# First batch's last three pairs of heads: token loads in 3072-byte pieces, with the cluster products taken by token parity

## The chip, the cores and the metric

The kernel runs on one core of a Trainium2 chip. A core has a matrix engine (TensorE, PE in the profile), a vector engine (VectorE, DVE), an engine for activation functions (ScalarE, ACT), a general engine (GpSimd, POOL), a queue engine that issues most DMA transfers (SyncE, SP), and sixteen DMA engines that all queues share. Each engine runs its own instructions strictly in order and waits for others by semaphores. The metric is the device time of one execution in microseconds; lower is better.

## The reference

Two stages follow each other. The first is attention in which a query sees only those keys that fall into its own cluster; the second is a feed-forward layer with a softmax-gated activation and a layer norm.

```python
batch, n_heads, seq, head_dim = (4, 8, 768, 64); n_clusters = 16
q_assign = np.argmax(np.einsum('bhsd,hcd->bhsc', q_n, c_n), axis=-1)
k_assign = np.argmax(np.einsum('bhsd,hcd->bhsc', k_n, c_n), axis=-1)
mask = q_assign[:, :, :, None] == k_assign[:, :, None, :]
scores = np.where(mask, scale * np.matmul(q, k.transpose(0, 1, 3, 2)), -1000000000.0)
attn = softmax(scores)
attn_out = np.matmul(attn, v)
x = attn_out.transpose(0, 2, 1, 3).reshape(B * S, H * D)      # 3072 x 512
h = x @ w_in                                                   # 3072 x 1024
solu = h * softmax(h)
ln = (solu - mu) / np.sqrt(var + 1e-06) * g_ln
return ln @ w_out                                              # 3072 x 512
```

All inputs and the output are 32-bit floats. q_n, k_n and c_n are the rows divided by their lengths.

## The kernel before

**Tiling.** The work is cut by batch (4) and by pairs of heads (4 in a batch), so there are 16 pairs; a name such as ca0.2.1.0 is a step, its batch, its pair, its side (0 for q, 1 for k) and a part. A pair's q and its k each fill one raw tile of 128 x 768 floats. What the attention needs is the transpose: the 64 head dimensions on partitions, the tokens as columns, in bf16, with 16 more rows below that hold each token's cluster as a one-hot column. These rows enter the same matrix product as the head dimensions, so that a score of a token pair from different clusters comes out so low that its exponential is nothing.

**The steps of a pair.** ld loads the raw tile. In the first batch (by_token) the six tokens of a partition lie beside each other and TensorE turns the tile by six 128x128 transposes into the region hreg (tp, L363), three a half; xa copies a half out of it (L370); in the other batches ld uses 128-byte pieces and VectorE turns 32x32 blocks (xt, L384). ca casts one head's 64 rows into the buffer qk (L400, L402, L404). cl multiplies the turned tile with the centroids (L413): four products that each write 32 rows of one output bank; the strips are q and k, first and second half of the tokens, and the weights c_bd hold both heads' centroids, zero outside their own head's rows. tb, mx, oh and ot (L422, L435, L440, L446) turn the result on VectorE, take the largest over 16 clusters, compare, and turn the one-hot columns back. pl puts them under both heads' columns of qk (L460, or L458 by a DMA), bl blanks 16 rows (L469). Then S makes the scores (TensorE, L539), E their exponentials (ScalarE, L545), V the sums over keys (L562), N divides (L587). The second stage is h (L648), its maximum hm, its exponential ex, the product u, statistics bn and ag, the transposes tx and tu by DMA, and y (L709).

**Before this stream.** The first pair of the first batch (halves_of) goes half by half, loaded ahead of everything else by SP and ScalarE. The centroids are normalised (cn), turned (cp, L796) and copied with a mask into c_bd (cb, L800). The weights of the second stage are loaded by lo and li, lo's are summed with the gains by VectorE (su, L514 and L517); their mean over 1024 rows is one matrix product (me, L522), which centres them (ce, L525). The values are loaded by lv and cast by cv (L478). fl are idle products that fill time.

**Order.** No scheduler decides the order of instructions. Every step is registered with a name, an engine, a cost and what it needs; for each engine a text (ORDER) lists the kinds of steps one after another, and each entry takes the next registered step of its kind on that engine. AWAY names the steps that run on another engine than their default. Both are long lists, and one change in them moves the whole order. Costs and the planned transfer times (move, lag) only decide in which order the engines' lists are merged as they are written out, not what an engine does first.

**Buffers that tie steps together.** raw has 8 tiles, xt 6, the scores' PSUM ring 3 banks, so that ScalarE can lag TensorE by three banks. hreg has three banks, used in turn by tp and later by h. One PSUM bank (tag m) is shared by cl, cp, the transpose of the gains (gt) and y: who takes it waits until it was read.

```python
eng.dma_start(out=tokens(b, p, i)[:, t0:t1, hh * D:(hh + 1) * D],
              in_=SRC[i][b, 2 * p + hh].rearrange("(p t) d -> p t d", p=P)[:, t0:t1, :])
```

This is the load of one head of the first batch: for each of 128 partitions six tokens in a row, but each token's 256 bytes go to a place of their own, since the other head's token lies between.

Of the kernel before, what the change touches and what calls it, by code (L numbers as in the profile page):

```python
# [22 lines left out]
class Weave:  # L23
# [6 lines left out]
        ld4 lv si ld11 lo lg ld lo lv ld2 lo ld3 lo ld2 lv ld3 lv ld3 li ld3 li2 ld2 li ld3 tx ld3  # L30
        lv ld3 lv ld5 tx2 lv tu ld3 tu ld lv ld9 tu ld4 lv ld6 tu2 ou2 tx lv ld3 tx ld tu ld ou lv
        tu ld6 ou ld7 tx ld5 ou ld2 lv ld2 ou ld6 ou tu ld4 tu2 lv ld pl2 tx ld2 ou ld lv2 tx lv pl
        tu2 pl tx ou2 pl3 tu2 ou tu ou tx2 tu ou tu tx tu ou tx tu ou tx ou2 tu ou tu2 ou6
    """
    ORDER["POOL"] = """
        po ca2 pl2 ca bl pl2 bl sg cv ca3 pl ca pl4 ca z bl z2 cv pl3 ca cv ca pl ca bl ca cv ca pl2
        ca pl cv pl ca cv ca cv pl2 ca wi pl wi z pl wi2 pl2 ca bl2 cv pl2 ca2 cv pl2 cv ca3 pl at z
        ca cv ca pl3 bl2 al at cv ca2 cv2 al pl ca pl ca at cv at ca3 pl3 al pl al ca6 at bl pl cv
        ca al pl3 cv2 at pl al ca2 bl ca pl2 at bl cv al pl ca at ca2 cv pl cv pl2 al pl at ca cv bl
        pl2 ca2 bl at ca3 al ca2 at cv at cv ca4 cv ca pl3 cv bl at pl al pl bl at al pl al at2 ca  # L40
        al pl cv at al2 at al3 at3 al2 at2 al2 at al2
    """
    ORDER["PE"] = """
        wm tp2 cp tp cl tp fl5 cl fl5 S3 tp S tp S2 tp2 S3 tp2 cl V tp2 V2 S3 cl S2 V3 S tp2 S2 gt
        S2 tp S2 V3 S2 tp S3 V S V S V S2 cl S3 V3 S2 V S2 V S V S4 V2 S V S2 V2 S2 V S2 me S2 V S
        V3 S2 V2 S3 cl S2 V S2 V2 S V2 S V S4 V S V3 S3 cl S3 V2 S V2 S3 V S2 V3 S2 h S h S2 h2 S3
        cl S V2 S V2 h V2 S h S2 h S h S2 V S V3 S V S V S h2 cl S2 h S h S2 V S V2 S h S2 V3 S2 y4
        S2 V2 S V2 S2 h V2 S2 h2 S2 y S V2 S y3 S3 V h2 S h S V h S V2 S2 h2 S2 V S V cl V2 S2 h V2
        S3 cl S2 V3 S2 V h S2 y S V2 S V2 S y S2 y2 h V S2 V h2 S V S h S2 h y S2 V y3 S2 V2 S h S
        V2 S V S h2 S2 V S cl h S V3 S2 h y V y S y S2 y V2 S h2 S3 V h V S y S y3 V3 h S V S2 y S y  # L50
        S2 V2 y S2 y S h V2 S2 h S V2 S2 cl S3 V2 cl h S2 V S V2 S h2 V S2 h S h S2 V cl V3 S2 V S y
        V y S3 y h S y V S V2 S2 y S V h S2 h S V2 S V2 S2 y2 S3 h2 V2 y S V2 S2 h3 S3 V h S V cl S2
        V2 S V cl S V S2 h S h V S V S y3 S2 V h V2 y S V S2 h S h S h S V2 S V S y2 h S y V2 y S V
        h S h3 S3 h V2 S2 V y S y2 V y V2 S2 h3 S3 V h y2 V y V S y V S3 h2 S V S V S y S V2 y S3 y2
        h2 S V h2 S3 h V y S V2 y3 S h S2 h V2 h S y S V2 y2 h S y S h V h S h S V S y V2 y S y S y
        h4 y4 h S h y4 S h2 V4 y3 ptx y h2 y h2 ptu2 y8 ptu2 y7
    """
    ORDER["DVE"] = """
        cn cb ca tb mx oh ot pl2 cv tb mx oh ot xa3 ca2 tb ca xa pl mx oh tb ot xa gk N su xa2 mx su
        oh xa ot N tb su3 mx N oh su3 N ot xt2 ce N ce bl xt tb mx oh ot N ce xt N ce4 tb N mx oh ot  # L60
        ce xt N xt hm tb mx u N oh ot hm xt2 u tb N mx oh hm bn2 ag bn ot N u xt bn N bn2 hm ag xt u
# [11 lines left out]
    """  # L73
    AWAY = {}
    AWAY.update(dict.fromkeys("""
        ca0.0.0.0.1 ca0.0.0.1.0 ca2.2.1.0 tu23.1 xa0.0.0.1 xa0.0.1.0 xa0.1.1.0 xa0.2.0.0 xa0.2.0.1
        xa0.2.1.1
    """.split(), "ACT"))
    AWAY.update(dict.fromkeys("""
# [90 lines left out]
def kernel(  # L170
# [176 lines left out]
    def halves_of(b, p):  # L347
        return (b, p) == (0, 0)
# [816 lines left out]
```

## Time and profile before

| | us |
|---|---|
| median of 3 runs | 229.61 (228.98 to 231.76) |
| profiled execution, device time | 230.08 |
| its span, first to last instruction | 227.7 |
| busy: TensorE, VectorE, ScalarE, GpSimd | 218.3, 198.0, 193.9, 131.4 |

The profiled execution thus has 2.4 us outside its span. Busy time of TensorE is that of pipelined matrix products, whose ends are modelled. Of the page's second part, which cuts the span into 40 slices of 5.7 us, three rows matter here: the busy tenths of TensorE, the clock that it was granted, and the share of the DMA engines.

```profile
PE   7997999999999999999999999999999999999993
...
PEclk9999799999999999999999999999999999999999
DMA  6999799999999989899989999599246317557513
```

The fifth slice, 22.8 to 28.5 us, has a granted clock of 0.7. The loads' shapes and what they took from issue to landing are in the page's last part; the rows with 192 KB are the loads of the first batch:

```profile
vf<-in_v_dram SPq DMA_DIRECT2D x16, 384.0 KB, 4.6
...
w_g<-in_moe_w_out_dram SPq DMA_DIRECT2D x4, 512.0 KB, 7.1
...
raw<-in_q_dram SPq DMA_DIRECT2D x6, 192.0 KB, 4.6
raw<-in_k_dram SPq DMA_DIRECT2D x6, 192.0 KB, 4.7
```

One line of the list of who waited for whom:

```profile
PE hreg L363 <- DMA raw<-in_k_dram: 1.9, 2, 1.4
```

This reads: TensorE stood before transposes of raw tiles for 1.9 us in total, two times, the longest 1.4 us, and what came last was a load of k.

### The profile page before, as it was taken

How to read it: one execution, taken by the hardware profiler on the slowest of the kernel's cores; microseconds unless marked ns; L12 is line 12 of the kernel's file. 1: busy time of each engine (PE TensorE's matmuls, PEld its weight loads, DVE VectorE, ACT ScalarE, POOL GpSimd, SP SyncE). 2: the span in 40 equal slices, each digit the busy share in tenths (PEclk: the TensorE clock that was granted, in tenths of full speed). 3: DMA queues.
4: the chain of work that ended last, by engine and by line, in shares of the span. 5: the costliest groups of instructions: out<-in, count | busy, mean ns of one | idle time of the engine just before them, and what ended most of it. 6: DMA issues, size and time to landing. Idle time of an engine off the chain costs nothing.

```text
span 227.7 us, 6584 instructions
## 1 busy us (share of the span) xinstructions
PE 218.3 (96%) x2404; PEld 149.1 (65%) x2404; DVE 198.0 (87%) x348; ACT 193.9 (85%) x376; POOL 131.4 (58%) x253
## 2 busy tenths in 40 slices
PE   7997999999999999999999999999999999999993
PEld 3554767666767866867667677766667676665552
DVE  2888689999999989999899997899997996988980
ACT  3776799999999999999998999999988897874462
POOL 2495596877775975598489084979542240141131
PEclk9999799999999999999999999999999999999999
DMA  6999799999999989899989999599246317557513
GB/s 154 253 227 279 158 243 210 232 192 191 189 186 164 200 132 208 194 200 217 190 143 208 181 208 166 107 199 198 53 140 124 96 32 156 137 120 210 156 69 121
DMA packets 133695, 38.95 MB, mean 171 GB/s; under 512 B 124376, under 2 KB 129184, under 8 KB 133664
## 3 DMA queue, kind: packets, MB, share of 16 engines
q1 hardware_dynamic: 131920, 38.01, 81.9%
q10 hardware_dynamic: 1744, 0.52, 0.9%
q8 instruction: 19, 0.31, 0.6%
q14 instruction: 12, 0.10, 0.1%
HBM read 23.11 MB, written 6.29 MB: 129 GB/s over the span
## 4 chain that ended last, share of the span: by engine, by line
PE 78%; DMA 5%; SPq 5%; issue 4%; ACT 4%; DVE 2%; ACTq 0%; DVEq 0%
PE sps L539 24%; PE hreg L648 18%; PE yps L709 16%; PE ops L562 13%; PE csc L413 4%; SPq L356 4%; ACT e L545 4%; DMA raw<-in_k_dram 3%; DMA out_dram<-y 1%; DMA raw<-in_q_dram 1%; PE hreg L363 1%; DVE y L726 0%; DVE nmax L654 0%; SPq L510 0%; DVE bs L676 0%
## 5 line engine op out<-in xcount | busy, mean ns | idle before, releaser
L545 ACT ACTIVATE e<-sps 128x512 bf16<-128x512 f32 (+1 forms) x294 | 151.5, 605 | 13.9 <-PE sps L539 13.0
L539 PE MATMUL sps<-qk 80*128 80x256 bf16 (+5 forms) x636 | 97.8, 265 | 1.8 <-POOL qk L460 0.4
L539 PEld LDWEIGHTS <-qk 96*128 96x128 bf16 (+1 forms) x636 | 61.2, 121 | 30.1 <-issue 10.4
L562 PEld LDWEIGHTS <-e 128*128 128x128 bf16 x1152 | 52.2, 98 | 10.3 <-issue 2.2
L562 PE MATMUL ops<-v,e 128*128 128x65 bf16 x1152 | 56.8, 194 | 0.0
L648 PE MATMUL hreg<-w_in_sb,xT 128*128 128x512 bf16 x192 | 53.1, 379 | 0.2 <-DVE xT L629 0.2
L709 PE MATMUL yps<-w_out_c,uT 128*128 128x512 bf16 x184 | 48.7, 378 | 0.0
L460 POOL COPY qk<-oht 32x384 f32<-32x384 f32 (+1 forms) x58 | 29.0, 499 | 32.2 <-DVE oht L446 24.1
L665 DVE TENSOR_TENSOR u<-e_sb,hreg 128x1024 bf16<-128x1024 bf16 x24 | 29.0, 1208 | 5.5 <-ACT e_sb L660 5.4
L660 ACT ACTIVATE e_sb<-hreg,nmax 128x1024 bf16<-128x1024 f32 x24 | 26.8, 1117 | 7.7 <-DVE nmax L654 6.0
L676 DVE BATCH_NORM_STATS2 bs<-u 128x6 f32<-128x512 bf16 x48 | 31.3, 675 | 0.2
L654 DVE TENSOR_REDUCE nmax<-hreg 128x1 f32<-128x1024 f32 x24 | 29.1, 1212 | 1.8 <-PE hreg L648 1.7
L402 POOL CAST qk<-xt 64x768 bf16<-64x768 f32 (+1 forms) x29 | 24.6, 849 | 6.1 <-ACT xt L370 3.4
L404 POOL TENSOR_SCALAR qk<-xt 64x768 bf16<-64x768 f32 (+1 forms) x30 | 25.2, 839 | 2.2 <-ACT xt L370 0.4
L709 PEld LDWEIGHTS <-uT 128*128 128x128 bf16 x200 | 17.9, 97 | 10.9
L648 PEld LDWEIGHTS <-xT 128*128 128x128 bf16 x192 | 16.8, 97 | 10.8 <-DVE xT L629 0.7
L384 DVE STREAM_TRANSPOSE xt<-raw 128x768 f32<-128x768 f32 x24 | 22.6, 956 | 0.0
L692 POOL TENSOR_SCALAR esq<-es,mv 128x1 f32<-128x1 f32 x24 | 8.2, 340 | 24.8 <-DVE mv L680 23.7
L587 DVE TENSOR_TENSOR x<-ops,den 128x384 bf16<-128x384 f32 (+1 forms) x37 | 18.6, 503 | 1.3
L478 POOL CAST v<-vf 128x384 bf16<-128x384 f32 x27 | 14.7, 549 | 4.6 <-PE ops L562 2.7
L686 POOL TENSOR_SCALAR es<-esum 128x1 f32<-128x1 f32 x24 | 5.2, 220 | 17.0 <-ACT e_sb L660 16.3
L695 POOL TENSOR_TENSOR alpha<-esq,halves 128x1 f32<-128x1 f32 x24 | 13.7, 571 | 2.0
(70 smaller groups left out, 164.7 us busy)
## 6 DMA issues: line engine op xcount, KB each, us to landing
vf<-in_v_dram SPq DMA_DIRECT2D x16, 384.0 KB, 4.6
out_dram<-y SPq DMA_DIRECT2D x23, 256.0 KB, 2.3
raw<-in_q_dram SPq DMA_DIRECT2D x50, 96.0 KB, 3.5
raw<-in_k_dram SPq DMA_DIRECT2D x50, 96.0 KB, 3.4
w_g<-in_moe_w_out_dram SPq DMA_DIRECT2D x4, 512.0 KB, 7.1
w_st<-in_moe_w_in_dram SPq DMA_DIRECT2D x4, 512.0 KB, 6.2
raw<-in_q_dram SPq DMA_DIRECT2D x6, 192.0 KB, 4.6
raw<-in_k_dram SPq DMA_DIRECT2D x6, 192.0 KB, 4.7
```

Of the source, the lines that this page charges most:

```text
L402: VEC[e].tensor_copy(dst, xt[r, cols])
L404: VEC[e].tensor_scalar(dst, xt[r, cols], scalar1=inv_C, scalar2=1.0, op0=Alu.mult, op1=Alu.mult)
L460: ins = VEC[e].tensor_copy(dst.bitcast(F32), src.bitcast(F32).unsqueeze(1) .to_broadcast([NB, 2, n // 2]))
L539: nc.tensor.matmul(sps_[n, k][:, c0:c0 + w], side(b, h // 2, 1, h % 2, keys)[r], side(b, h // 2, 0, h % 2, slice(s0 * P, s0 * P + w))[r])
L545: nc.scalar.activation(es[n, k][:, :w], sps_[n, k][:, :w], Act.Exp, scale=exp_scale, bias=-exp_scale)
L562: nc.tensor.matmul(opss[g][:, s, :VW], es[n, k][:, c0:c0 + P], v1[slot(b, h // 2)][:, h % 2, kt, :VW], start=(kt == 0), stop=(kt == n_t - 1))
L648: uses(nc.tensor.matmul(hreg[:, at(f, f2)[1], :], xTs[f][:, dc, :], w_in_sb[:, dc, f2 * FF2:(f2 + 1) * FF2], start=(dc == 0), stop=(dc == ...
L654: uses(nc.vector.tensor_reduce(ff[f, "nmax"][:], pair_of(f), axis=AXY, op=Alu.max, negate=True), *both(f))
L660: uses(nc.scalar.activation(ff[f, "e"][:], pair_of(f), Act.Exp, bias=ff[f, "nmax"][:], accum_out=ff[f, "esum"][:]), *both(f))
L665: uses(nc.vector.tensor_tensor(ff[f, "u"][:], ff[f, "e"][:], pair_of(f), op=Alu.mult), *both(f))
L676: nc.vector.bn_stats(ff[f, "bs"][:, f2, :], ff[f, "u"][:, f2, :])
L709: ins = nc.tensor.matmul(dst, ff[f, "uT"][:, at(f, f2)[0] * (n_fc // 2) + c, :], w_out_c[:, fc, cols], start=(fc == 0), stop=(fc == n_fc - 1))
```

## The change

For pairs 1, 2 and 3 of the first batch (twelve), the token tile is laid out in another way. Both heads' tokens go twelve by twelve on 64 partitions each, so that a partition's 3072 bytes are one run in memory and in the tile, and a side needs one load of 384 KB where it had two of 192 KB. A transpose of 128 columns now turns two neighbouring tokens of both heads: the rows that come out are token parity and head dimension, the columns are head and partition.

```diff
+    def load_twelve(b, p, i):
+        raws[b, p, i] = ld.tile([P, n_j, NB], F32, name="raw")
+        nc.sync.dma_start(out=raws[b, p, i][:].rearrange("p j c -> p (j c)"),
+                          in_=SRC[i][b, 2 * p:2 * p + 2].rearrange("h (q t) d -> (h q) (t d)",
+                                                                   q=D))
+    def by_two(b, p, i):
+        return xts[b, p, i][:].rearrange("p (h t n) -> p h t n", h=2, t=n_t // 2)
```

The copy out of hreg (xa) puts every column at every other place, so that the order of tokens in qk stays what it was. A cast (ca) now takes one parity of both heads and writes every other block of 128 columns; so the scores of either head need all four casts of their pair.

```diff
+        if twelve(b, p):
+            dst = by_two(b, p, i).rearrange("p h t (q u) -> p h t u q", u=2)[:, :, :, hf, :]
+            src = src.rearrange("p (t h q) -> p h t q", h=2, q=D)
...
+    def every_other(b, p, i, part):
+        return (qk[slot(b, p)][:, i * 2 * S:(i + 1) * 2 * S]
+                .rearrange("p (h t n) -> p h t n", h=2, t=n_t)[:, :, part::2, :])
...
+        if twelve(b, p):
+            src, dst = by_two(b, p, i)[r], every_other(b, p, i, hh)[:D]
```

The strips of the cluster product are now q and k, even and odd tokens. A strip sums two products, one for each head, with weights that are zero but for the rows of one parity and the columns of one head; there are eight products where there were four.

```diff
+        if twelve(b, p):
+            for hh, c in ((hh, c) for hh in range(2) for c in range(4)):
+                i, part = divmod(c, 2)
+                nc.tensor.matmul(csc[c * NB:(c + 1) * NB, :], c_by_two[:, p, 2 * part + hh, :],
+                                 by_two(b, p, i)[:, hh].rearrange("p t n -> p (t n)"),
+                                 start=(hh == 0), stop=(hh == 1), tile_position=(0, c * NB))
```

These weights, c_by_two, lie in the tile of the second stage's weights, which is not yet in use, and are made by a second transpose of the centroids (cq) and a product with a mask (cf), ahead of which GpSimd writes the mask with five memsets:

```diff
+    nc.gpsimd.memset(own_two, 0.0)
+    for part in range(2):
+        for hh in range(2):
+            nc.gpsimd.memset(own_two[part * D:(part + 1) * D, 2 * part + hh,
+                                     hh * NC_:(hh + 1) * NC_], 1.0)
...
+    def keep_by_two():
+        nc.vector.tensor_tensor(
+            c_by_two, cs["t"][:].rearrange("p a h c -> p a (h c)").unsqueeze(2)
+            .to_broadcast([P, n_pair, 4, 2 * NC_]),
+            own_two.unsqueeze(1).to_broadcast([P, n_pair, 4, 2 * NC_]), op=Alu.mult)
+    add("cq", "PE", 0.28, 0, lambda e: turn_centroids(), ["cn"], ["cp"], take="m")
+    add("cf", "DVE", 0.65, -490, lambda e: keep_by_two(), ["cq"], give="m")
```

Placing (pl) writes every other block as well, on GpSimd or VectorE.

ORDER and AWAY are new throughout, for all five engines and all batches. What they move in the first stretch, by name:

- SP: the six loads come first, with lv0.1 ahead of the last and lv0.2 ahead of lo0; lo0 to lo3 come after them, among the loads of batch 1. In all nine placings go by DMA (seven before).
- TensorE: cq stands ahead of the first scores S0.0; cl0.1 behind tp0.2.1.0, cl0.2 ahead of V1.0 and S2.0, gt ahead of tp0.3.0.0; from S3.0 to me the order is nearly what it was.
- VectorE: xa0.0.0.0, xa0.2.0.1, cf, cv0.1.1, pl0.1.0.1 and pl0.2.0.0 come to it; ca0.0.1.1.1 and ca0.2.0.0 leave it; ot0.3 stands ahead of su4 (before: behind su7).
- ScalarE: xa0.0.0.0 and xa0.2.0.1 leave it; ca0.1.0.0 comes to it, between E0.4 and E0.5; the first pair's casts stand ahead of and behind xa0.0.1.1.
- GpSimd: it has 208 steps in all where it had 218; cv0.0.0 stands ahead of the first placing.

More of the change, by code (lines that the diff above doesn't have):

```diff
@@ L46 @@
[L46 to L50, printed above, removed]
```

140 lines of the change are left out of this document (78 added, 62 removed).

## The prediction, on record before the changed kernel ran

> **What bounds the kernel now.** I read the page first, then the chain that ended last in order of time, then windows and the timeline of the first 40 us, where every edited step lies.
>
> ```profile
> PE 218.3 (96%) x2404; PEld 149.1 (65%) x2404; DVE 198.0 (87%) x348; ACT 193.9 (85%) x376; POOL 131.4 (58%) x253
> ```
>
> TensorE is the engine that the end stands on. Its idle time before raw tiles and its slow clock both lie early. The chain names the place:
>
> ```profile
> 12.87 0.79 SPq L356
> 13.71 1.02 SPq L510
> 15.23 6.54 DMA raw<-in_k_dram
> 21.91 0.78 PE hreg L363 x3
> ...
> 28.18 0.78 PE csc L413 x8
> ...
> 37.80 0.94 PE hreg L522 x2
> ```
>
> (start, us, what.) SP issues the token loads one by one at 0.65 to 0.9 us each; the last one, issued at 15.23 behind a weight load, takes 6.54 us to land, and TensorE starts its transpose only at 21.91. The windows (engines' busy us, granted clock, DMA share, GB/s) show what it cost:
>
> ```profile
> 12.00:16.00 4.00, 3.52 (x44) 2.29 (x42) 3.27 (x5) 2.74 (x8) 3.79 (x7) 1.00 1.32 220
> 16.00:20.00 4.00, 4.00 (x46) 2.37 (x43) 3.90 (x9) 3.23 (x8) 1.63 (x3) 1.00 1.11 318
> ...
> 20.50:21.00 0.50, 0.01 (x1) 0.00 (x0) 0.32 (x1) 0.50 (x3) 0.46 (x2) 1.00 1.10 341
> ...
> 22.00:22.50 0.50, 0.50 (x4) 0.44 (x5) 0.00 (x0) 0.00 (x0) 0.50 (x1) 0.53 0.37 67
> ...
> 25.00:25.50 0.50, 0.50 (x4) 0.43 (x3) 0.00 (x0) 0.50 (x2) 0.34 (x1) 0.55 1.19 200
> ```
>
> While 256-byte pieces are loaded the queue moves 220 GB/s at a full share; with 2048-byte weight rows in it, 318. TensorE stands from 20.51 to 21.91 (1.40 us) and then runs at half clock to 25.45, 3.45 us. So what the late load costs is 1.40 + 3.45/2 = 3.1 us. Two more windows, and VectorE's and ScalarE's rows:
>
> ```profile
> 14.80:37.60 22.80, 20.60 (x244) 14.56 (x242) 19.07 (x34) 18.12 (x40) 16.54 (x26) 0.93 0.94 222
> 26.00:58.00 32.00, 30.55 (x398) 21.62 (x400) 29.60 (x52) 31.07 (x63) 25.34 (x38) 1.00 0.96 201
> ```
>
> ```profile
> 14.82 0.58 DVE L422 STREAM_TRANSPOSE cst<-csc 128x384 f32<-128x384 f32 x1 [0.50 <-PE csc L413]
> ...
> 29.11 0.58 DVE L422 STREAM_TRANSPOSE cst<-csc 128x384 f32<-128x384 f32 x1 [0.88 <-PE csc L413]
> ...
> 34.11 3.45 DVE L517 SCALAR_TENSOR_TENSOR w_sum<-w_g,g_ln,w_sum 128x512 f32<-128x512 f32 x3
> ```
>
> From 26 to 58 us ScalarE is busy 31.07 of 32 and VectorE 29.60: the exponentials set the pace there, and VectorE has little to spare. After 60 us TensorE is back to back to 224. A time that is won before 26 us therefore reaches the end only if neither VectorE nor ScalarE gives it back before 58.
>
> **The change, part by part.** *Loads.* Twelve loads of 192 KB become six of 384 KB, with pieces of 3072 bytes. The first may be issued at 4.03 as now, behind the first value load that lands at 7.60. 2.36 MB at 220 GB/s take 10.7 us, at 330 (between 318 and the 341 of the rows) 7.2. One value load (0.39 MB) now stands ahead of the sixth, so the last one lands near 7.6 + 2.75/0.33 = 15.9, against 21.78. If 3072-byte pieces were as slow as 256-byte ones: 7.6 + 2.75/0.22 = 20.1, still before TensorE would ask for them. The weight loads slip behind two value loads: 2.36 + 0.79 + 0.52 MB put the first at 18.7 (now 21.0), before its reader on VectorE. So the 1.40 us wait goes in either case; what is late next is not a DMA.
>
> *Cluster products.* Each of the three pairs has eight products in place of four, 16 records in place of 8. The chain prices the eight at 0.78, so +0.78 a pair, 2.34 in all on TensorE (bounds 0.5 and 0.85 a pair: the four strips run together now, and a record of a cold group took 0.85). All three lie before 30 us, in the stretch in which ScalarE waits for scores; at cl0.3 ScalarE has three banks of scores in hand (about 1.4 us of work), and its gap there, 0.34 us now, grows to some 0.8.
>
> *Second centroid transpose and its copy.* cq costs what the first does, 0.27 us, but it takes the one-bank pool that tb0.0.1 frees, and it stands ahead of the first scores. ScalarE also does the second half's copy behind two 0.52 us casts, so cl0.0.1 moves from 7.80 to about 8.5. First scores: 9.43 becomes about 9.95, +0.5 (bounds 0 and 0.9). cf on VectorE is a 512-element product from PSUM; the 128-element one took 0.29 and a 512-element row 0.49 to 0.74: 0.65. The five memsets on GpSimd (0.21 for 128x128 and four of 0.1) fit in its idle 0.94 us before c_s.
>
> *Strided copies.* xa writes every other float, the casts write every other block of 128, the placing writes six blocks of 64 words in place of two of 192. No row has these patterns. Bounds: as the contiguous rows (0.54, 0.86, 0.51), or half as much again; below nothing is excluded, since the element counts are the same. I take the contiguous rows: the runs stay long, but for xa, which reads PSUM anyway. Upper price: ten VectorE xa x 0.27 = 2.7 us on a queue with little slack, kept for the range. Scores of a pair's first head now need all four casts: now the last of pair 1 ends at 15.81 and its first score runs at 25.59, so that is covered.
>
> *Moved steps.* VectorE between tb0.1 and the end of the weight sums (14.82 to 37.56, 19.07 busy) gets one value cast (0.44), two placings (0.6 each, between the 0.41 and 0.70 of its rows) and ot0.3 (0.56), while it loses one copy (0.53); casts balance. Net +1.7 (1.4 to 2.3). SP gets nine placings in place of seven, late, and six fewer issues early. ScalarE takes one full cast (0.84) among the first exponentials, where it now idles 1.26 us before its copy at 15.78, and two more after 100 us, where TensorE is the one without idle time: nothing for these, 0.84 each if that cover is gone.
>
> **The sum.** Through the first pair: +0.5 late start; then the missing 0.48 us wait at 13.10 pays for part of cl0.1, and tb0.1 begins near 15.3. The scores behind cl0.2 and the values come about 1.2 us later than now at 17.6, but nothing stands still at 20.5 and the clock stays up, so the first exponential of pair 1 moves from 26.18 to about 24.1: 2.1 won. At cl0.3, 0.45 goes back: 1.65. VectorE, without the 3.7 us in which it now idles, ends the weight sums at 15.3 + 20.8 = 36.1 against 37.56: 1.5. The mean product (37.64 now) stands in TensorE's order ahead of the next scores and waits for that sum, so the lesser counts, and I round down to 1.2 for idling that I can't see. Behind it both orders hold the same TensorE work, so 1.2 us reach the end. The profiled execution took 230.08 (span 227.7 and 2.4 around it), 0.47 over the median of 229.61; on the median: **228.4 us**.
>
> **The rivals.**
> *VectorE becomes the bound (slower).* Its queue must hold cf, two more PSUM copies and two placings, and the weight sums on it hold up the mean product and every score behind it. It breaks even where tb0.1 to the sums takes 22.3 us. With strided placings at 0.9 and a slower copy or two (+1.5) and 0.5 us of idling left, it ends at 38.1 to 38.4; with the start 0.5 late and the cluster gap that makes +0.9: 230.5. For it: 29.60 of 32 busy. Against it: 3.7 us idle that the earlier loads give back.
> *The clock drops again (slower to level).* 1.40 us of standing still were followed by 3.45 us at 0.53 to 0.55. In the new order TensorE waits for tb0.2 ahead of gt and for banks around cl0.2; if that is enough, 1.7 us go: 229.6 + 0.5 = 230.1. The Trainium skill, TensorE: Matmul & The Clock Gate, section Why this matters for your kernels, says that only a gap of about 3 us brings the clock down. By that rule the time would stay at 228.4; the trace disagrees, with 1.40 us.
> *All 3.1 us come through.* If VectorE keeps up and the products of two strips overlap: 226.5. Against it: the 2.34 us of new products.
> *The change does not do what it says:* the loads stay at 220 GB/s. The last then lands at 20.1, as worked out above, but the earlier ones no sooner than now, and the 0.48 us wait at 13.10 stays: 228.9, inside the forecast's own range.
>
> **How the numbers follow.** Forecast (227.2 to 229.5) 0.46, VectorE 0.24, clock 0.10, all 3.1 us 0.13, something dearer by 4 us or more (strided forms at half as much again everywhere, 2.7 + 1.3) 0.07. The likeliest gives 228.4. 226.1 to 231.6 takes in all but the last case and the outer halves of the neighbours, 0.8. A difference under 2% (4.6 us) is about what can't be told from no change here: faster 0.04 (below 225.0 the gain would have to exceed the 3.1), same 0.88, slower 0.08.
>
> **What would show it.** Last token load landed by 17 and no raw releaser before TensorE's transposes after 13 us; granted clock 1.00 in 20:30; cluster groups of 16 records at 1.5 to 1.6 us; first scores at 9.9; the first exponential of pair 1 near 24; mean product near 36.3 with VectorE as releaser. The forecast is wrong if the weight sums end after 37.6, if the clock row shows another stretch at 0.5, or if stretches after 60 us, which I take as equal, differ by over 1 us.

## The result and the profile after

Over 20 executions each on one chip, the changed kernel took 229.75 us (median; 228.82 to 231.27) and the kernel before 228.7 us (227.17 to 231.76): a ratio of 1.006, with a 95% interval of 1.004 to 1.008. It is slower by 0.6%, where the forecast had it faster by 0.5%. The profiled execution of the changed kernel took 230.84 us, its span 228.7. Ratios here and below leave out the executions that took over 1.5% longer than the fastest of their kernel (among them five of the twelve of b_ld_lg_first, and three that took 365 to 756 us), while the medians hold all executions.

Four rows of the page of the changed kernel: busy time, the granted clock in 40 slices, and the two groups of token loads with what they took from issue to landing.

```profile
PE 219.9 (96%) x2429; PEld 149.5 (65%) x2429; DVE 200.0 (87%) x354; ACT 195.4 (85%) x379; POOL 126.0 (55%) x248
...
PEclk9999999999999999999999999999999999999999
...
raw<-in_q_dram SPq DMA_DIRECT2D x3, 384.0 KB, 6.0
raw<-in_k_dram SPq DMA_DIRECT2D x3, 384.0 KB, 6.5
```

The clock row has no 7 any more, and the 384 KB loads land in about 6 us each. The windows of the changed kernel that answer to those shown of before (span of time; length, then busy us of TensorE, its weight loads, VectorE, ScalarE, GpSimd; granted clock, DMA share, GB/s):

```profile
12.00:16.00 4.00, 4.00 (x37) 3.25 (x39) 3.69 (x8) 3.98 (x11) 2.70 (x10) 1.00 1.05 399
...
20.50:21.00 0.50, 0.50 (x7) 0.15 (x3) 0.50 (x2) 0.12 (x1) 0.44 (x2) 1.00 0.81 291
22.00:22.50 0.50, 0.50 (x6) 0.47 (x5) 0.50 (x2) 0.50 (x3) 0.44 (x2) 1.00 1.05 393
...
14.80:37.60 22.80, 21.19 (x275) 13.96 (x274) 21.29 (x39) 19.34 (x42) 16.50 (x27) 1.00 1.01 237
26.00:58.00 32.00, 29.51 (x397) 20.99 (x395) 30.53 (x54) 30.00 (x61) 26.92 (x38) 1.00 0.79 171
```

The loads do what the change says: 399 GB/s in 12:16 where there were 220, the last token load landed at 15.37 (before: 21.78), TensorE does not stand at 20.5 and keeps its clock. VectorE is busy 21.29 of the 22.80 us from 14.8 to 37.6, 2.2 more than before. Three pieces of the chain of waits (start, us, what) and a line of what TensorE waited for (total, times, longest):

```profile
15.55 1.47 PE csc L440 x16
...
28.08 1.23 DVE w_sum L554
29.44 0.56 DVE x L624
```

```profile
PE ops L599 <- DVE x L624: 1.2, 2, 0.7
```

The cluster group of 16 records takes 1.47 us on the chain. The values wait twice for a normalisation (x) that stands behind weight sums on VectorE. None of that explains why the change is slower: the profiled span is 1.0 us longer than before, although the first exponential of pair 1 comes at 25.56 us where it came at 26.18.

### The profile page after: what moved, and what is told of

The parts are those of the page before. It is cut to its first block, busy times and chain, and to the rows that moved or that the text cites. A ratio compares the mean times of both kernels' runs of the same rounds, so it can differ in the third digit from the quotient of the medians.

```text
span 228.7 us, 6646 instructions
## 1 busy us (share of the span) xinstructions
PE 219.9 (96%) x2429; PEld 149.5 (65%) x2429; DVE 200.0 (87%) x354; ACT 195.4 (85%) x379; POOL 126.0 (55%) x248
## 4 chain that ended last, share of the span: by engine, by line
PE 76%; DVE 13%; issue 4%; ACT 3%; DMA 2%; POOL 0%; DVEq 0%; ACTq 0%
PE sps L576 22%; PE hreg L685 16%; PE yps L746 16%; PE ops L599 11%; PE csc L445 4%; ACT e L582 3%; PE hreg L378 2%; DVE xt L402 2%; DMA out_dram<-y 2%; DVE w_sum L554 1%; DVE cst L454 1%; DVE bs L713 1%; DVE x L624 1%; DVE xt L388 1%; DMA c_all<-in_centroids_dram 1%
## 5 line engine op out<-in xcount | busy, mean ns | idle before, releaser
L576 PE MATMUL sps<-qk 80*128 80x256 bf16 (+5 forms) x636 | 96.8, 264 | 2.1 <-ACT e L582 0.5
L599 PEld LDWEIGHTS <-e 128*128 128x128 bf16 x1152 | 50.2, 97 | 12.4 <-issue 1.9
L599 PE MATMUL ops<-v,e 128*128 128x65 bf16 x1152 | 54.2, 193 | 1.2 <-DVE x L624 1.2
L685 PE MATMUL hreg<-w_in_sb,xT 128*128 128x512 bf16 x192 | 54.0, 379 | 0.0
L497 POOL COPY qk<-oht 32x384 f32<-32x384 f32 (+1 forms) x44 | 21.7, 492 | 32.3 <-DVE oht L478 26.2
L428 POOL CAST qk<-xt 64x768 bf16<-64x768 f32 (+1 forms) x27 | 22.3, 825 | 6.5 <-ACT xt L388 4.0
L430 POOL TENSOR_SCALAR qk<-xt 64x768 bf16<-64x768 f32 (+1 forms) x28 | 24.1, 861 | 2.0
L761 ACT ACTIVATE y<-yps,alpha 128x512 f32<-128x512 f32 x16 | 11.1, 696 | 4.7 <-PE yps L746 1.9
L515 POOL CAST v<-vf 128x384 bf16<-128x384 f32 x26 | 13.4, 522 | 1.0
```

What stands on the lines that cost most here:

```text
L428: VEC[e].tensor_copy(dst, src)
L430: VEC[e].tensor_scalar(dst, src, scalar1=inv_C, scalar2=1.0, op0=Alu.mult, op1=Alu.mult)
L576: nc.tensor.matmul(sps_[n, k][:, c0:c0 + w], side(b, h // 2, 1, h % 2, keys)[r], side(b, h // 2, 0, h % 2, slice(s0 * P, s0 * P + w))[r])
L599: nc.tensor.matmul(opss[g][:, s, :VW], es[n, k][:, c0:c0 + P], v1[slot(b, h // 2)][:, h % 2, kt, :VW], start=(kt == 0), stop=(kt == n_t - 1))
L685: uses(nc.tensor.matmul(hreg[:, at(f, f2)[1], :], xTs[f][:, dc, :], w_in_sb[:, dc, f2 * FF2:(f2 + 1) * FF2], start=(dc == 0), stop=(dc == ...
```

## The experiments

No kernel below leaves out a part of the work. They ran in five groups, each on one chip beside executions of the kernel before: the first four after the top row, then four, four, four and two, with 12 executions of each unless said otherwise. The ratio is to the kernel before, with its 95% interval. The other columns come from one profile each: when the first scores (S0.0) and the first exponential of pair 1 (E4.0) started, and how long it took from the start of exponential E30.0, near 68 us, to the end of the span.

| kernel | median us | ratio | S0.0 | E4.0 | E30.0 to end |
|---|---|---|---|---|---|
| before, first profile | 229.61 | | 9.43 | 26.18 | 158.76 |
| b_again | 229.89 | 0.9988 (0.9952 to 1.0024) | 9.81 | 23.54 | 158.87 |
| a_again | 230.33 | 1.0045 (1.0016 to 1.0075) | 10.70 | 24.73 | 159.27 |
| b_ld_first | 229.24 | 0.9994 (0.9969 to 1.0018) | 9.81 | 24.60 | 158.68 |
| a_dve | 230.05 | 1.0027 (0.9996 to 1.0059) | 10.00 | 23.96 | 161.33 |
| old_order | 228.88 | 0.9977 (0.9956 to 0.9997) | 9.40 | 23.82 | 159.19 |
| b_cl8 | 229.99 | 1.0047 (1.0019 to 1.0076) | 9.60 | 24.35 | 159.07 |
| a_wm8 | 230.46 | 1.0054 (1.0026 to 1.0082) | 10.21 | 24.16 | 159.55 |
| b_ld_lg_first | 230.00 | 0.9986 (0.9943 to 1.0029) | 9.67 | 23.42 | 159.00 |
| early_old (10) | 230.81 | 1.0098 (1.0059 to 1.0136) | 9.94 | 24.37 | 161.28 |
| late_old | 229.04 | 1.0014 (0.9989 to 1.0038) | 10.20 | 24.14 | 158.90 |
| start_old | 229.75 | 1.0045 (1.0017 to 1.0073) | 9.82 | 24.41 | 160.34 |
| old_again | 228.32 | 0.9993 (0.9968 to 1.0018) | 9.40 | 23.82 | 159.02 |
| early_old_h6 | 230.58 | 1.0073 (1.0040 to 1.0106) | 9.51 | 23.94 | 161.64 |
| a_h6 | 230.36 | 1.0067 (1.0039 to 1.0095) | 10.18 | 24.13 | 161.43 |
| old_h6_tight | 228.69 | 1.0022 (0.9989 to 1.0054) | 9.71 | 24.13 | 159.25 |
| old_h12 | 228.36 | 0.9994 (0.9967 to 1.0021) | 9.88 | 24.30 | 159.09 |
| early_old_h6_ou (6) | 230.83 | 1.0102 (1.0059 to 1.0146) | 9.84 | 24.11 | 162.32 |
| a_ou | 229.31 | 1.0038 (1.0015 to 1.0060) | 10.30 | 24.25 | 159.67 |
| changed, first profile | 229.75 | 1.0060 (1.0040 to 1.0080) | 11.60 | 25.56 | 159.76 |

A letter stands for a theory or rival as its own expectation words it; the same letter can mean another thing elsewhere. Medians of different groups do not compare directly: the kernel before itself took 229.41, 229.52, 228.67, 228.56 and 228.48 in the five groups.

**Both kernels again.** No edit: the question was whether the profiles of the prediction and of the result were typical.

> The kernel before, unchanged, to see how its start and its clock differ from run to run. Theory A (the profiled run of before was an unlucky one: in most runs the 1.40 us wait for the last token load does not bring the clock down): runs that show a clock of 0.995 or more take some 1.7 us less than those at 0.99, they are the larger part, and a new profile has no stretch at half clock between 20 and 26 us. Theory B (the stretch at half clock is there in nearly every run, and the changed kernel loses elsewhere): clock near 0.991 in nearly all runs, and a new profile shows 0.5 again after the wait.

> The changed kernel, unchanged. Its first profile has the idle products between 8 and 10.4 us at twice their distance (0.21 us instead of 0.11) and its first scores at 11.60 instead of 9.43. Theory A: that start is a matter of the run, as the times fall into two groups about 1.2 us apart (229.2 to 229.9 and 230.4 to 231.3); a new profile may show the first scores near 10.0 with the products 0.11 us apart, and then a span about 1.2 us shorter. Theory C (the change itself brings the slow start, by the transfers that now run beside the first loads): first scores at 11 us or later again, and all runs alike.

b_again, the kernel before once more: lines of what TensorE waited for, and a window of the same execution.

```profile
PE hreg L648 <- DMA xT<-x: 1.8, 1, 1.8
...
PE hreg L363 <- DMA raw<-in_k_dram: 0.7, 2, 0.4
...
PE gps L504 <- DMA g_rows<-in_moe_g_ln_dram: 0.3, 1, 0.3
```

```profile
55.00:60.00 5.00, 5.00 (x31) 2.50 (x30) 2.43 (x3) 3.10 (x6) 1.76 (x4) 0.72 1.03 208
```

The wait of 1.4 us for the last raw tile was not there: TensorE waited 0.27 us for that tile and at most 0.4 us for any k tile, no slow clock followed, and E4.0 came at 23.54, 2.64 us earlier than in the profile that the prediction read. That execution lost its time elsewhere, at 52 us, with 1.80 us of waiting for a transposed tile and then a lower clock (0.72 in 55:60, 1.00 in the first profile). Of the 155 executions of the kernel before in all groups, 9 have a mean granted clock of 0.992 or less, as the first profile had (0.991). So a slow stretch of that size belongs to about one execution in seventeen, and a median does not contain it. This is theory A. a_again gives 1.0045 on this chip, so the loss is there again. Its profile starts slowly too, though less so (first scores at 10.70 us), and its span of 227.5 us is 1.2 us shorter than the first one's, as theory A had it.

**The late load alone.** One load moved in the kernel before, then a second one with it.

```diff
- SP: ... lo0 lg ld0.3.1 lo1 ...
+ SP (b_ld_first):    ... ld0.3.1 lo0 lg lo1 ...
+ SP (b_ld_lg_first): ... ld0.3.1 lg lo0 lo1 ...
```

> The kernel before with one edit: the last load of the first batch's tokens is issued ahead of the first weight load, not behind it. It should land near 18.2 us (0.9 us behind the one at 17.33) instead of 21.78, so TensorE's 1.40 us wait is gone, and any drop of the clock that came of it, with no cluster product and nothing on VectorE added. Theory B (wait and clock together, 3.1 us, at hand in every run): ratio 0.987 to 0.990. Theory A (only the wait of 1.4 us at hand in a usual run, part of it given back to VectorE's queue): ratio 0.993 to 0.999.

> The kernel before with the last token load and the load of the gains ahead of the first weight load on SP. If the wait for the gains (1.2 us when only the token load was moved) is what gave the gain of the earlier load back, TensorE stands still for less than 0.3 us between 13 and 30 us, the first exponential of pair 1 comes at 23.0 to 23.6, and the ratio is 0.990 to 0.996. If 50 to 60 us (a wait for a transposed tile of the second stage) or the exponentials take back whatever is won early, the ratio is 0.997 to 1.001.

b_ld_first, what TensorE waited for:

```profile
PE gps L510 <- DMA g_rows<-in_moe_g_ln_dram: 1.2, 1, 1.2
```

The tile came at 18.34, and TensorE then stood 1.2 us for the next transfer, the gains, which the move had put one place further back. With the gains moved as well that wait is gone and E4.0 comes at 23.42, the earliest of all profiles. Neither is faster beyond its interval: 0.1 and 0.3 us, with up to 1.3 us of gain left open for the second, whose median over all twelve executions even lies 0.5 us above before's. Removing the late load is not worth 3.1 us in typical executions.

**The doubled cluster products alone.** In the kernel before, each of the three pairs' four products issued twice; the second four write the same sums again.

```diff
-        for c in range(4):
+        for c in [*range(4)] * (2 if b == 0 and p else 1):
```

> The kernel before with the four cluster products of pairs 1, 2 and 3 of the first batch issued twice; the second four write the same sums again, so only their time is added. Theory A: each group of records grows from 0.78 to 1.5, 2.2 us in all on TensorE, and 0.8 to 1.6 us of it reach the end: 230.2 to 231, ratio 1.003 to 1.007. Rival B (new lists) and rival C (start): the products lie beside other work and cost nothing, ratio 0.998 to 1.002.

b_cl8, timeline of TensorE (start, busy us, line, op, output and inputs, form, count):

```profile
14.02 1.50 PE L413 MATMUL csc<-xt,c_bd 128*32 128x384 f32 x16
```

Each group took 1.50 us as in the changed kernel, and the ratio is 1.0047: 1.1 us of some 2 reach the end. As theory A had it, the products are not hidden.

**The layout under the lists of before.** The changed kernel's functions with before's ORDER and AWAY: the late load is behind lo0 again, cq behind the second pair's transposes, cf after that pair's copies.

```diff
-        ld4 lv si ld5 lv ld lg lv lo ...        (SP, new)
+        ld4 lv si ld5 lo lg ld lo lv ...        (SP, as before)
-        wm tp2 cp tp cl tp fl5 cl fl5 cq S3 tp2 S2 ...                  (TensorE, new)
+        wm tp2 cp tp cl tp fl5 cl fl5 S3 tp S tp S2 tp2 cq S3 ...       (TensorE, as before)
```

> The changed layout (loads, products, copies, casts and placings of the three pairs) with the engines' lists of before: the last token load again behind the first weight load, cq behind the second pair's transposes, cf on VectorE after the second pair's copies, all other steps in before's order and on before's engines. Theory A (the layout itself costs: 2.3 us of new cluster products, and nothing is won for them, since the wait of 1.4 us and the slow clock behind it are absent from most executions): 229.5 to 231, ratio 1.003 to 1.010, first exponential of pair 1 between 24.5 and 25.5. Rival B (the new lists cost, not the layout): 228 to 229.3, ratio 0.994 to 1.000, that exponential before 24.0. Rival C (the start at half pace costs): first scores near 10 here, as the second transpose of the centroids no longer stands ahead of them, and ratio about 1.001.

> The changed layout with before's lists throughout, unchanged from its first run (228.88, ratio 0.9977), to see whether that holds on another occasion: 228.5 to 229.2, ratio 0.995 to 1.000, with all executions under 230. If the first run was luck, ratio 1.001 to 1.006.

Theory A falls and rival B holds: with before's lists the layout takes 0.9977 and 0.9993 of before, a little faster or level, and the same layout with the new lists 1.006 and 1.0045. old_again came as expected in its ratio and its longest execution (229.66 us); its median of 228.32 us is a little below the range named. The lists, which the change has renewed for all batches, cost about 0.68% (1.0053 against 0.9985, the means of two ratios each), 1.5 us. From b_cl8 to old_order on one chip the ratio goes down by 0.7%, 1.6 us: that is what everything else in the layout wins back. The last token load lands at 15.69 us in old_order and at 20.51 in b_cl8, but no run separates the loads from the rest.

**The start.** In the changed kernel's first profile TensorE is slow until about 10 us, and the clock row does not show it. Changed kernel, timeline of TensorE:

```profile
8.48 1.27 PE L791 MATMUL idle_p<-w_out_c 128*128 128x256 bf16 x5
...
11.60 0.66 PE L576 MATMUL sps<-qk 80*128 80x384 bf16 x3 [0.30 <-DVE qk L497]
```

Five idle products of 256 columns take 1.27 us; in the warm case they take 0.71. In a_wm8 eight idle products in place of six close the gap ahead of the first transposes; in start_old TensorE, VectorE, ScalarE and GpSimd follow before's order for the first 13 us.

```diff
-    add("wm", "PE", 3.55, -1000, lambda e: [idle(FF2) for _ in range(6)])
+    add("wm", "PE", 3.55, -1000, lambda e: [idle(FF2) for _ in range(8)])
```

> The changed kernel with eight idle products at the start in place of six, so that TensorE has work until about 4.8 us and no gap stands between them and the first transposes. Rival C (in the changed kernel the products before 10 us run at half pace in most executions, 0.21 us for an idle product of 256 columns in place of 0.11): here the idle products behind the first pair's transposes come 0.11 apart, first scores at 10.0 to 10.6, and the time falls by 0.7 to 1.2 us against the changed kernel, ratio to before 0.999 to 1.002. Theory A and rival B: the two products only move the start, first scores at 10.3 to 11.6, ratio 1.003 to 1.007.

> The changed kernel with before's order for the first 13 us alone on TensorE (34 steps; cq goes behind the second pair's transposes), VectorE (18), ScalarE (17) and GpSimd (13), and the new lists for the rest and for SP throughout. If the start is what costs: first scores at 9.4 to 9.9 in place of 10.0 to 11.6, idle products of 256 columns 0.11 apart, and 228.7 to 229.3, ratio 0.996 to 1.000. If the normalisations on VectorE or anything later costs: first scores as early, but 229.6 to 230.4, ratio 1.002 to 1.006.

a_wm8, timeline of TensorE:

```profile
1.17 3.59 PE L791 MATMUL idle_p<-w_out_c 128*128 128x512 bf16 x8 [1.17 <-DVE halves L795]
...
7.75 0.71 PE L791 MATMUL idle_p<-w_out_c 128*128 128x256 bf16 x5
...
10.21 0.66 PE L576 MATMUL sps<-qk 80*128 80x384 bf16 x3
```

Both starts were warm and first scores came at 10.21 and 9.82, and the ratios stayed at 1.0054 and 1.0045. So the slow start, which two of the six profiles with that start have, is real but does not decide the time: rival C falls.

**VectorE's queue.** In the changed kernel one placing and one value cast go from VectorE to GpSimd, and the normalisations N1 and N2 stand ahead of a weight sum and of a placing.

```diff
+ pl0.1.0.1: DVE -> POOL, behind pl0.1.0.0      cv0.1.1: DVE -> POOL, behind cv0.1.0
+ DVE: N1 ahead of su1, N2 ahead of pl0.2.0.0
```

> The changed kernel with VectorE's queue relieved: one placing and one value cast of pair 1 go back to GpSimd (1.4 us less on VectorE before 26 us), and the divisions of the second and third group stand ahead of the weight sum and the placing behind which they waited (TensorE stood 0.88 and 0.66 us for them). Theory D (VectorE's queue between 17 and 38 us is what the changed kernel loses by): weight sums end about 1.4 us earlier, the mean product with them, and the time is 1.0 to 1.5 us below the changed kernel's: ratio to before 0.999 to 1.002 where the changed kernel has 1.006. Rival E (the loss lies in the late start and the doubled cluster products): within 0.4 us of the changed kernel, 1.004 to 1.007.

The mean product came at 36.74 and V4.0 at 27.58. The changed kernel's first profile has 38.70 and 30.06, but with a slow start; a_h6, a_ou and late_old, which share its lists there and started warm, have 37.28 to 37.38 and 28.63 to 28.74, so the edit moved them by 0.6 and 1.1 us where theory D had 1.4 for the sums. The ratio is 1.0027 (0.9996 to 1.0059), between the ranges of D and E, and can't be told from the changed kernel's 1.0045 on the same chip. In its profile what had been won by 30 us was lost behind it (161.33 us from E30.0 to the end), 1.15 us of it in one wait for a transposed tile at 97.5 us.

**The lists cut at 60 us.** All with the changed layout: each engine takes from one set of lists what starts in the first 60 us, and the rest in the order of the other.

```diff
+        x, y = self.listed(self.ORDER_X, self.AWAY_X), self.listed(self.ORDER_Y, self.AWAY_Y)
+        early = {i for e, q in x.items() for i in q[:self.CUT[e]]}
+        queues = {e: x[e][:self.CUT[e]] + [i for i in y[e] if i not in early] for e in x}
```

> The changed layout with the lists of before for what starts in the first 60 us (60 steps on SP, 192 on TensorE, 85 on VectorE, 104 on ScalarE, 70 on GpSimd) and the new lists for the rest. Theory B1 (the new lists cost in the first 60 us: a start at half pace, and normalisations that stand behind placings and weight sums on VectorE and hold up the values): the kernel is as fast as the changed layout under before's lists throughout, 228.5 to 229.2, ratio 0.995 to 0.999. Rival B2 (the new lists cost behind 60 us, by waits for transposed tiles): 229.6 to 230.5, ratio 1.002 to 1.007.

> The reverse: the changed layout with the new lists for what starts in the first 60 us (60 steps on SP, 183 on TensorE, 84 on VectorE, 101 on ScalarE, 68 on GpSimd) and before's lists for the rest. Theory B1: the loss of the changed kernel is all here, 229.7 to 230.5, ratio 1.003 to 1.007, and the first exponential of pair 1 comes at 24.0 to 25.5. Rival B2: 228.5 to 229.2, ratio 0.995 to 0.999.

B1 falls: old lists early and new ones late take 1.0098, new ones early and old ones late 1.0014. That is B2's order, but neither ratio lies in the range that B2 had named (1.002 to 1.007, and 0.995 to 0.999). The early lists seem to cost a little too (1.0014 against old_again's 0.9993; the intervals overlap), and the splice of old and new costs more than the new lists throughout. The last column of the table goes the same way: in the ten profiles with old lists behind 60 us E30.0 to the end took 158.68 to 159.25, in the ten with the new ones 159.27 to 162.32. The changed kernel's own two profiles, 159.76 and 159.27, lie just above the old range; the long ones are of edited kernels. Windows of old_again, of early_old and of the changed kernel:

```profile
110.00:120.00 10.00, 10.00 (x107) 7.11 (x105) 8.79 (x15) 9.41 (x19) 8.03 (x15) 1.00 0.88 149
120.00:130.00 10.00, 10.00 (x128) 7.17 (x126) 9.83 (x15) 9.42 (x19) 4.12 (x7) 1.00 0.96 206
```

```profile
110.00:120.00 10.00, 9.42 (x99) 6.01 (x92) 9.37 (x16) 8.51 (x16) 4.98 (x9) 1.00 1.06 221
120.00:130.00 10.00, 10.00 (x120) 7.14 (x116) 7.83 (x13) 9.95 (x21) 7.98 (x15) 1.00 1.00 182
```

```profile
110.00:120.00 10.00, 9.51 (x99) 6.06 (x93) 9.40 (x16) 8.59 (x16) 4.92 (x9) 1.00 1.12 238
```

With the old lists TensorE is busy throughout and ScalarE has 0.6 us of slack in each 10. In early_old ScalarE stands 1.5 us in the first window and is full in the second (9.95), so that it can't make it up, and TensorE stands 0.6 us. The changed kernel's first profile has nearly the same (8.59, and TensorE 9.51), a_again less of it (9.28 and 9.89).

The new lists also give ScalarE more to do there: two casts (ca) of a whole side of a head, where the old lists have one. ScalarE's timeline in the changed kernel, then in old_again:

```profile
112.65 0.83 ACT L426 ACTIVATE qk<-xt 64x768 bf16<-64x768 f32 x1
...
121.88 0.84 ACT L426 ACTIVATE qk<-xt 64x768 bf16<-64x768 f32 x1
```

```profile
107.69 0.84 ACT L426 ACTIVATE qk<-xt 64x768 bf16<-64x768 f32 x1
```

From E30.0 to E60.0 ScalarE is busy 59.3 us in both profiles of the changed kernel and 58.8 in old_again. No run moved the second cast back, so what it costs is not shown.

**Which place in the late lists.** In early_old TensorE waited 0.67 us at 97.7 for a tile turned by DMA, which in the new lists h6.0.0 asks for just as it lands. early_old_h6 and a_h6 put three other steps first; old_h6_tight takes the margin away under the old lists; old_h12 gives the old lists more margin at a second such place.

```diff
+ PE (early_old_h6, a_h6): y2.3 S46.0 S46.1 ahead of h6.0.0
+ PE (old_h6_tight):       y2.2 y2.3 behind h6.0.0
+ PE (old_h12):            V68.0 V68.1 y8.3 ahead of h12.0.0
```

> As the kernel with before's lists for the first 60 us and the new lists behind them (ratio 1.0098), but with one product of the second stage and two of scores (y2.3, S46.0, S46.1, some 0.9 us) put ahead of h6.0.0 on TensorE, which in the new lists asks for a tile turned by a DMA transpose just as it lands. Theory H (that wait is what the late lists cost, because ScalarE has no slack behind it to catch up): 228.6 to 229.6, ratio 1.000 to 1.004, and no wait for the transposed tile near 97 us. Rival E (the late lists are slower by the order of exponentials and scores between 100 and 131 us, whether h6 waits or not): 230.3 to 231, ratio 1.007 to 1.011.

> The changed kernel with the same three steps put ahead of h6.0.0. Theory H: 228.9 to 229.5 beside 229.7 to 230.3 for the changed kernel, ratio 0.998 to 1.003. Rival E: ratio 1.004 to 1.007 as without the edit.

> The reverse: the changed layout under before's lists, with y2.2 and y2.3 (0.9 us) moved from ahead of h6.0.0 to behind it, so that h6.0.0 asks for its tile 0.9 us earlier, about 0.4 us before it lands. Theory H: 0.4 us or more are lost, ratio higher than without the edit (0.9977, 0.9993) by 0.002 to 0.005, so 1.000 to 1.004. Rival E: the wait is made up behind it, ratio 0.997 to 1.000.

> The changed layout under before's lists with V68.0, V68.1 and y8.3 (0.8 us) put ahead of h12.0.0, which waited 0.3 to 0.8 us for its transposed tile near 146 us in every profile under these lists. If such waits reach the end: 0.3 to 0.7 us faster than 228.3 to 228.9, ratio 0.995 to 0.998, better than both kernels. If not: 0.998 to 1.000.

The wait at h6 was gone in both kernels, with 0.34 us at 97.8 for a bank of scores in its place, and the ratios stayed high: 1.0073 and 1.0067. The changed kernel's own two profiles show at most 0.3 us of waiting there. Theory H falls as the main cause. Under the old lists the lost margin gave 1.0022, where theory H had it, though its interval also holds one of the unedited kernel's two ratios, 0.9993. With the added margin the wait for the tile near 146 us was gone, but TensorE stood 0.45 us there for a normalisation, and the ratio of 0.9994 is no gain. But the profile of a_h6 shows what ScalarE waits for between 75 and 125 us, and its timeline and SP's show the place:

```profile
ACT y L767 <- DMA out_dram<-y: 1.5, 1, 1.5
```

```profile
115.75 0.69 ACT L767 ACTIVATE y<-yps,alpha 128x512 f32<-128x512 f32 x1 [1.53 <-DMA out_dram<-y]
```

```profile
106.93 1.27 SPq L713 DMA_TRANSPOSE uT<-u  x1
108.25 0.57 SPq L400 DMA_DIRECT2D raw<-in_q_dram  x1
108.88 2.68 SPq L400 DMA_DIRECT2D raw<-in_k_dram  x4
111.60 0.53 SPq L400 DMA_DIRECT2D raw<-in_q_dram  x1
112.23 1.85 SPq L779 DMA_DIRECT2D out_dram<-y  x2
```

ScalarE's sc4 writes into a buffer that the output transfer ou2 must have emptied. ou2's rows were ready near 101, but SP issued it at 112.23, behind the transpose and the six loads shown, among others. Under the old lists ou2 goes out at 100.79. In the changed kernel's own two profiles sc4 also starts 0.1 us after ou2 has landed, but the wait is 1.16 us in the first and 0.23 in a_again. The row of the first names another releaser:

```profile
115.60 0.69 ACT L761 ACTIVATE y<-yps,alpha 128x512 f32<-128x512 f32 x1 [1.16 <-POOL alpha L732]
```

GpSimd's alpha had ended at 113.38 there, and ou2 landed at 115.50. The transfer ou2 was then moved ahead of lv2.2, in the changed kernel alone (a_ou) and in early_old_h6.

```diff
- SP: tx8 ld3.0.0.2 lv2.2 pl2.1.0.0 tu5 ld3.0.0 ... ld3.1.0.0 ou2 ou3
+ SP: tx8 ld3.0.0.2 ou2 lv2.2 pl2.1.0.0 tu5 ld3.0.0 ... ld3.1.0.0 ou3
```

> The changed kernel with ou2 ahead of lv2.2 on SP and nothing else. Theory O: no wait over 0.4 us on ScalarE near 114, 0.5 to 1.2 us faster than the changed kernel, ratio 1.000 to 1.004. Rival E: 1.004 to 1.007.

> As the kernel with before's lists early, the new lists late and h6.0.0 moved (ratio 1.0073), with one more step moved: the output transfer ou2, which in the new lists is issued on SP near 112 us, behind six loads and two transposes, though its rows are ready at 101, goes ahead of lv2.2 (near 105). Theory O: ScalarE's sc4 stands 1.2 to 1.5 us near 114 for the buffer that this transfer empties, TensorE then waits for score banks at 117, and ScalarE has no slack to catch up; with the edit that wait is below 0.3 us, ScalarE is busy over 9.2 of 10 in 110:120, and the ratio is 1.000 to 1.004. Rival E (nothing but the order of scores and exponentials): 1.006 to 1.009 as without the edit.

a_ou, SP's timeline, ScalarE's, and a window:

```profile
104.21 0.52 SPq L779 DMA_DIRECT2D out_dram<-y  x1
```

```profile
113.45 0.69 ACT L767 ACTIVATE y<-yps,alpha 128x512 f32<-128x512 f32 x1 [0.22 <-POOL esq L735]
```

```profile
110.00:120.00 10.00, 10.00 (x111) 7.01 (x109) 9.22 (x17) 9.71 (x18) 5.81 (x11) 1.00 1.03 213
```

The wait is 0.22 us, ScalarE is busy 9.71 of 10 and TensorE 10.00, and the ratio is 1.0038 (1.0015 to 1.0060), at the upper end of what theory O had named and close to rival E's 1.004. Without this edit the changed kernel and its versions a_again, a_wm8, start_old and a_h6 have 1.0045 to 1.0067, a_dve 1.0027. The intervals overlap with a_ou's, and a_again had a wait of only 0.23 us without the edit, so a gain is not shown. In early_old_h6_ou the wait fell to 0.58 us and the ratio of 1.0102 is above both ranges. There TensorE waited for two other transfers of SP's queue between 75 and 130 us:

```profile
PE sps L655 <- DMA qk<-oht: 0.9, 1, 0.9
PE yps L825 <- DMA uT<-u: 0.5, 1, 0.5
```

So theory O describes its one place rightly, and it is not the whole cause.

## Why the prediction was wrong

**Loads** (right). The last one landed at 15.37 (forecast 15.9), raw tiles released no wait after 13 us, and the DMA engines moved up to 399 GB/s.

**Cluster products** (right). 1.50 us a group, 0.65 to 0.72 more than four took, where 0.78 had been taken. b_cl8 puts what reaches the end at 1.1 us.

**Start** (wrong in size in some executions). First scores at 9.95 were forecast, within 0 to 0.9 us of extra. They came at 11.60 and 10.70 in the two profiles with a slow TensorE, and at 10.00 to 10.30 in the four with a warm one. It did not set the time (a_wm8, start_old).

**Strided copies** (right). Copies, casts and GpSimd's placings took what the contiguous rows take (0.55, 0.82, 0.50 us); the placings on VectorE took 0.88 and 0.96 where 0.6 had been taken.

**What the late load costs, 3.1 us** (mis-sized). The sum compared a forecast of the new order with one profiled execution of the old one. For the new order it was good: E4.0 was forecast near 24.1, and the profiles with a warm start have 23.96 to 24.25. But the old order has 23.54 where the profile had 26.18. The step that failed is "so the first exponential of pair 1 moves from 26.18 to about 24.1: 2.1 won": in the second profile of before, the changed kernel comes 0.4 to 0.7 us later, not 2.1 earlier. The clock's share of the 3.1 us (1.7) belongs to some 6% of the executions. What the layout wins besides its doubled products measured 1.6 us (old_order against b_cl8).

**VectorE's weight sums, 1.5 us won** (wrong). The step "ends the weight sums at 15.3 + 20.8 = 36.1 against 37.56" took the same atypical profile for its baseline, and its own side came out too short. The mean product, which waits for the sums, began at 37.28 to 37.38 us in the warm profiles with the changed kernel's early lists (36.3 forecast) and at 35.19 in b_again (37.64 in the first profile): about 2.1 us later, not 1.3 earlier. From the end of the cluster group ahead of tb0.1 to the mean product it took 21.7 us in the changed kernel and in a_h6. VectorE was busy for 21.1 of them, where the forecast had 20.8 in all.

**"Behind it both orders hold the same TensorE work, so 1.2 us reach the end"** (wrong). This step took renewed lists at nothing because the work was the same. late_old and early_old put the cost of the lists behind 60 us above that of the lists ahead of it: 0.2% early (late_old against old_again), 0.3 to 0.5% late (start_old's 1.0045 and the changed kernel's 1.006 against late_old), and 1.05% late in the spliced early_old (against old_again). The text had named this as what would make it wrong, stretches after 60 us that differ by over 1 us: from E30.0 to the end the ten profiles with new lists take 160.7 us in the mean and the ten with old ones 159.0, though the unedited changed kernel's two are only 0.3 and 0.8 above that. "The same TensorE work" also looked at one engine alone: behind E30.0 the new lists hold three more steps on ScalarE (239 against 236). The prediction put the casts that ScalarE takes after 100 us at "nothing for these, 0.84 each if that cover is gone". From 120 to 130 us ScalarE is busy 9.95 of 10 in both profiles of the changed kernel, so there it has no idle time to take them in; how much they cost was not measured.

Put together from these measured terms: 1.6 won by the layout, 1.1 lost to the products, some 1.5 lost to the lists, 1.0 us slower; 1.0 to 1.4 was measured in two groups. The three terms are steps from one kernel to the next, so that they add up proves nothing beyond the steps. The forecast had -3.1, about +1.9 for products, start and VectorE, and 0.

**The rivals.** VectorE as the bound is half right: it does hold up the values by 1.2 us and the mean product came at 38.70, not 36.3. With a warm start it comes at 37.28 to 37.38, still 1.0 us late, but relieving VectorE (a_dve) does not clearly give the loss back. The clock did not drop again in the changed kernel's two profiles. The row had shown a drop after 1.40 us of standing still; b_again has one after 1.80 us (0.72 in 55:60) and none after 0.3, and waits of 1.17 us in b_ld_first and 1.15 us in a_dve were followed by none. The Trainium skill (TensorE: Matmul & The Clock Gate, section Why this matters for your kernels) puts the limit at about 3 us. Both traces of before disagree with it. No rival was the mechanism that decided: that the order far behind the edited stretch had changed as well.

**What stays open.** That the late lists cost is shown, most clearly by early_old against old_again on one chip. What in them costs is not settled. The profiles show transfers that SP issues too late between 75 and 125 us: an output near 112 in the changed kernel, and in its edited versions also a transposed tile at 97 and placings and a turned product near 79, 86, 111 and 123. Taking one away may have helped in one kernel and did not in the other, and no kernel was tried with all of them mended. ScalarE's second cast in that stretch is a rival that no run tests. No version beats the kernel before by more than its interval twice: old_order did once (0.9977) and not again (0.9993).

## What to carry to other kernels

Before a stall in one profiled execution is priced, look whether a second execution has it: its price in the median is its price times how often it occurs. When a change comes with a new order for the whole program, price the order too, by running the change under the old order and the two orders cut at some point, and look far behind the edited stretch at what one queue must deliver and who has no slack to wait. Add up the work behind the edit for every engine, not for the one that was the bound. A transfer that frees a buffer can be as urgent as one that fills it.

## What the hardware showed that was not expected

TensorE can run at half pace while the clock row reads 1.00, as it does from 8 to 10 us in the changed kernel's first profile. At the start, 256-column products came 0.21 us apart until about 10 us in two of six profiles of the same start and 0.11 apart in the others. The Trainium skill (TensorE: Matmul & The Clock Gate, section Part 1: The HAM clock gate) has both paces, as 1.2 and 2.4 columns a nanosecond, and says that when the clock rises depends on a free-running window, so that it differs from run to run; the six profiles agree that it differs.

An order can be stable or not. From E30.0 to E60.0 nine of the ten profiles with old lists took 60.46 us to within 0.01, the kernel before among them, and one (old_h6_tight) 60.84. With the new lists, which hold 0.7 us more TensorE work in that stretch by the kernel's own costs, it took 61.3 to 64.6 us, never twice the same. Most of these ten are differently edited kernels, but the two profiles of the unedited one also differ: 61.75 and 61.32 us.
